# A kernel of attention and experts at its turn to the experts: a step of the softmax changes engine, four steps change place

## The chip, the cores and the metric

The kernel runs on one core of one Trainium2 chip. The metric is the device time of one execution in microseconds (us); three runs gave a median of 504.72 us (504.45 to 505.11). A core has TensorE (PE in the rows; PEld is its weight load), VectorE (DVE), ScalarE (ACT), GpSimd (POOL) and SyncE (SP), each with its own list of instructions, and 16 DMA engines.

## What is computed

Three stages follow one another: linear attention with decay over 2 x 768 tokens and 8 heads of 64; a dense layer `g = h * sigmoid(1.702 h)` between 512 and 2048 columns; and a mixture of 8 experts with one expert for each token. The change lies in the third:

```python
logits = xn @ en.T / tau                 # xn, en: rows scaled to length 1
expert_idx = np.argmax(logits, axis=1)
probs = np.exp(logits - logits.max(-1, keepdims=True))
probs /= probs.sum(-1, keepdims=True) + 1e-09
gate_w = probs[np.arange(N), expert_idx]
for e in range(E):                       # 8 experts, 512 -> 1024 -> 512
    mask = expert_idx == e
    h = np.maximum(x[mask] @ w1[e], 0.0)
    out[mask] = gate_w[mask, None] * (h @ w2[e])
```

## The kernel before

Tokens stand in tiles of 128 rows, twelve in all. All matrix products are made from a high and a low part of each operand (three products for one). The program order of each engine is written out by hand (`manual_schedule`): an engine takes its instructions in the order in which the functions issue them, and waits at an instruction whose operands are not there yet, with all that stands behind it.

Each tile of the dense layer's result is routed. `Batch` does this for one tile, or for two at once (b01, b23, b4 and b5 are the batches of the last six tiles):

- `norm` (L630 to L640): ScalarE squares the row, GpSimd takes the root. `rn` and `pick` (L672 to L706), on VectorE: logits `lg`, maximum, `z`, and the one-hot choice `oh`.
- `tanh` (L708) on ScalarE: the exponential is taken as (1 + t) / (1 - t) with t = tanh(z / 2).
- `gate` (L711): `dn = 1 - t` (L716), its reciprocal (L717), the sum and its reciprocal, which is written beside the token's row (L727).
- `rank` (L729): TensorE counts with `ltri` and `ones` how many tokens chose the same expert earlier (`pr`; it needs `oh`, and the counter `acc` of the batch before), VectorE makes from it the slot `pos`, adds to `acc` (L746) and casts the slot to an integer `pi` (L748).
- `scatter` (L750): GpSimd writes the token's row to its slot in DRAM with an indirect DMA.

`load_slots` (SP) reads the slots of one expert when all scatters have landed, and `emit_xT` (L892) transposes them on TensorE, ScalarE copies the high part (L901), VectorE makes the low part (L902). Expert 0 comes in two pieces: piece 0 has the tokens of the first six tiles and is loaded early, piece 1 the rest. `emit_mm1t` (L922) and `emit_mm2` (L991) are its two products: 12 and 24 matmuls of 512 columns for a piece and a half or a whole; `emit_relut` (L933, `hr`) and `emit_hT` (L940) stand between them.

`emit_tail` interleaves the last tiles of the dense layer, the routing of b01 to b5 and the first product of piece 0, so that TensorE has work while VectorE routes. The last scatter (b5) decides when piece 1 can be loaded; `emit_experts` goes on with the second product of piece 0 meanwhile.

Of the kernel before, what the change touches and what calls it, by code (L numbers as in the profile page):

```python
# [11 lines left out]
I32 = mybir.dt.int32  # L12
U32 = mybir.dt.uint32
AF = mybir.ActivationFunctionType
ALU = mybir.AluOpType
SYNC_DATA = mybir.DependencyInfo(mybir.DependencyClass.Sync, mybir.DependencyReason.DATA)

P = 128
# [33 lines left out]
def attn_moe_moe_kernel(  # L52
# [16 lines left out]
    nc = tc.nc  # L69
# [20 lines left out]
    def psum_h(shape, name):  # L90
        return ps.tile(shape, F32, tag="h", name=name)
# [158 lines left out]
    pos = {}  # L250
# [366 lines left out]
    class Batch:  # L617
# [93 lines left out]
        def gate(self):  # L711

            z = self.z
            dn = self.tile("dn", [P, self.n, E])
            sm = self.tile("sm", [P, self.n])
            nc.vector.tensor_scalar(dn, z, -1.0, 1.0, op0=ALU.mult, op1=ALU.add)  # L716
            nc.vector.reciprocal(dn, dn)  # L717
            if self.n == 1:
                nc.vector.scalar_tensor_tensor(
                    z, z, 1.0, dn, op0=ALU.add, op1=ALU.mult, accum_out=sm  # L720
                )
            else:
                nc.vector.scalar_tensor_tensor(z, z, 1.0, dn, op0=ALU.add, op1=ALU.mult)
                nc.vector.tensor_reduce(sm, z, axis=mybir.AxisListType.X, op=ALU.add)
            nc.vector.tensor_scalar(sm, sm, 1e-9, None, op0=ALU.add)
            for j, i in enumerate(self.ts):
                nc.vector.reciprocal(yrow[self.g, i][:, DM:DM + 1], sm[:, j:j + 1])  # L727

        def rank(self):  # L729
            pr = psum_h([P, self.n, E], f"pr{self.tag}")  # L730
            for j in range(self.n):
                nc.tensor.matmul(pr[:, j, :], ltri, self.oh[:, j, :], start=True, stop=False)
                for before in range(j):
                    nc.tensor.matmul(
                        pr[:, j, :], ones, self.oh[:, before, :], start=False, stop=False
                    )
                nc.tensor.matmul(pr[:, j, :], ones, acc, start=False, stop=True)
            pf = self.tile("pf", [P, self.n, E])
            pos = self.tile("pos", [P, self.n])
            for j in range(self.n):  # L740
                nc.vector.scalar_tensor_tensor(
                    pf[:, j, :], pr[:, j, :], 0.0, self.oh[:, j, :], op0=ALU.add, op1=ALU.mult,
                    accum_out=pos[:, j:j + 1],
                )
            for j in range(self.n):
                nc.vector.tensor_tensor(acc, acc, self.oh[:, j, :], op=ALU.add)  # L746
            self.pi = self.tile("pi", [P, self.n], I32, bufs=4)
            nc.vector.tensor_copy(self.pi, pos)  # L748

        def scatter(self):  # L750
            for j, i in enumerate(self.ts):
# [88 lines left out]
    def split_e(e, kind, n):  # L840
        split_h(e, kind, n)
        split_l(e, kind, n)
# [35 lines left out]
    def tiles(e):  # L878
        return [(0, W - P), (W - P, P)] if e == 0 else [(0, P), (P, SLOTS[e] - P)]
# [34 lines left out]
    def emit_mm1t(a, half, lo=0, hi=None):  # L914
        off, n = tiles(0)[a]
        x = xe[0][:, 2 * KD * off:2 * KD * (off + n)].rearrange("p (k l w) -> p k l w", k=KD, l=2)
        if lo == 0:
            mm1ps[a, half] = (psum_h if a else psum_y)([P, DM], f"m1t_{a}_{half}")
        steps = [(k, s) for k in range(KD) for s in ((0, 0), (1, 0), (0, 1))]
        last = len(steps) - 1  # L920
        for i, (k, (xi, wi)) in list(enumerate(steps))[lo:hi]:
            nc.tensor.matmul(  # L922
                mm1ps[a, half][0:n], x[:, k, xi, :],
                ws[0, 0, k][wi][:, half * DM:(half + 1) * DM],
                start=(i == 0), stop=(i == last),
            )
# [243 lines left out]
    def emit_tail():  # L1170
        rest = list(range(NF - DEFER, NF))
        last = TPG - 1
        b01, b23, b4, b5 = Batch(1, 0, 1), Batch(1, 2, 3), Batch(1, 4), Batch(1, 5)
        where = {0: (b01, 0), 1: (b01, 1), 2: (b23, 0), 3: (b23, 1), 4: (b4, 0), 5: (b5, 0)}
        for i in range(TPG):
            emit_l2(1, rest, i, 0, 5)
            if i == 1:
                emit_xT(0, 0)
            if i > 2:
                b, j = where[i - 1]  # L1180
                b.transpose(j, KD)
            if i == last:
                b23.pick()
                b23.tanh()
                b01.rank()
                b01.scatter()
            emit_l2(1, rest, i, 5)
            emit_y(1, i)
            b, j = where[i]
            b.norm(j)  # L1190
            if i < 2:
                for e in range(E):
                    b01.dot_dve(i, e)
            if i == 4:
                b23.dots_pe()
                b01.rn()
                b01.pick()
                b01.tanh()
                b01.gate()
                b23.rn()  # L1200
        b23.gate()
        b23.rank()
        b23.scatter()
        b4.rn()
        b4.dots_pe()
        b5.transpose(0, KD)
        b4.pick()
        b4.tanh()
        b5.rn()
        emit_mm1t(0, 0, 0, 6)  # L1210
        b4.gate()
        b5.dots_pe()
        b4.rank()
        b4.scatter()
        for n in (2, 3):
            split_h(0, 1, n)
        b5.pick()
        b5.tanh()
        emit_mm1t(0, 0, 6)
        emit_relut(0, 0)  # L1220
        emit_mm1t(0, 1, 0, 4)
        b5.gate()
        b5.rank()
        b5.scatter()
        load_slots(0, 1)
        emit_mm1t(0, 1, 4, 6)
        emit_hT(0, 0)
        split_l(0, 1, 2)
        emit_mm1t(0, 1, 6)
        emit_relut(0, 1)  # L1230

    def emit_experts():
        emit_mm2(0, 0, 0, 6)
        emit_hT(0, 1)
        split_l(0, 1, 3)
        emit_places()
        load_slots(1)
        for n in range(4):
            load_e(1, 0, n)
        for n in range(4):  # L1240
            load_e(1, 1, n)
        emit_mm2(0, 0, 6, 18)
        emit_xT(0, 1)
        emit_mm2(0, 0, 18)
        emit_out(0, 0)
        emit_mm1t(1, 0)
        emit_relut(1, 0)
        emit_mm1t(1, 1, 0, 6)
        emit_hT(1, 0)
        split_e(1, 0, 0)  # L1250
        emit_mm1t(1, 1, 6)
        emit_relut(1, 1)
        for n in range(4):
            load_e(2, 0, n)
        for e in range(E):
            more = e + 1 < E
            if e:
                parts = [(n, i) for n in range(1 if e == 1 else 2, 4) for i in range(2)]
                for f in range(NEF):
                    emit_mm1(e, f)  # L1260
                    if f == 0 and e == 1:
                        emit_out(0, 1)
                    emit_sum(e, f)
                    if f == 0 and e > 1:
                        emit_out(e - 1, 1)
                    if f:
                        emit_relu(e, f - 1)
                    if 1 <= f <= len(parts):
                        split_h(e, 1, *parts[f - 1])
                    if 1 < f <= len(parts) + 1:  # L1270
                        split_l(e, 1, *parts[f - 2])
                    if e == 3 and f == 6:
                        emit_ctl()
                emit_relu(e, NEF - 1)
                if e + 2 < E:
                    for n in range(4):
                        load_e(e + 2, 0, n)
            if more:
                for a in range(NA):
                    emit_xT(e + 1, a)  # L1280
                if e + 2 < E:
                    load_slots(e + 2)
            if e == 0:
                emit_mm2(0, 1, 0, 6)
                emit_hT(1, 1)
                for n in range(1, 4):
                    split_e(1, 0, n)
                split_e(1, 1, 0)
                emit_mm2(0, 1, 6)
            else:  # L1290
                for n in range(4 if more else 0):
                    split_e(e + 1, 0, n)
                emit_mm2(e, 0)
                emit_out(e, 0)
                for n in range(2 if more else 0):
                    split_e(e + 1, 1, n)
                emit_mm2(e, 1)
            if e + 2 < E:
                for n in range(4):
                    load_e(e + 2, 1, n)  # L1300
        emit_out(E - 1, 1)
# [201 lines left out]
```

## Time and profile before

| | |
|---|---|
| median of three runs | 504.72 us (504.45 to 505.11) |
| the profiled execution, its own time | 504.72 us |
| its span, first to last instruction | 503.0 us |
| TensorE busy | 490.8 us (98%) |
| VectorE busy | 356.9 us (71%) |
| ScalarE busy | 268.6 us (53%) |
| GpSimd busy | 108.5 us (22%) |

TensorE is busy through nearly the whole span, so what it waits for is what a change can give or take; the other engines matter where TensorE waits for them. Matmuls overlap in the records (one of 512 columns shows 0.39 us, and the next starts 0.23 to 0.24 us after it), so the step between starts says more than the busy time. The turn to the experts lies between 308 and 346 us.

### The profile page before, as it was taken

What the parts mean: (1) busy time and instruction counts of PE and PEld (TensorE: products, weight loads), DVE (VectorE), ACT (ScalarE), POOL (GpSimd) and SP (SyncE); (2) the same over time, 40 slices, a digit from 0 to 9 for tenths busy, and PEclk for the clock granted to TensorE, in tenths of its full rate; (3) what the DMA queues carried; (4) which work ended last, traced back from release to release, by engine and by line L of the source; (5) the groups of instructions that cost most, each with busy time, mean ns of one, the idle gap of its engine ahead of it and who ended that gap; (6) DMA issues with size and microseconds to landing.
All of it is one profiled execution on the core that took longest, in us unless ns stands there. A gap on an engine that the chain in (4) does not pass through costs nothing. (4 is left out here: it accounts for less than half of the span.)

```text
span 503.0 us, 9454 instructions
## 1 busy us (share of the span) xinstructions
PE 490.8 (98%) x3479; PEld 424.1 (84%) x3480; DVE 356.9 (71%) x850; ACT 268.6 (53%) x576; POOL 108.5 (22%) x153
## 2 busy tenths in 40 slices
PE   8999999999999999999999999999999999999993
PEld 5888898898898899898989988778797988879781
DVE  6788877777687335988789478748956878676640
ACT  2463554554533476434354574538856678567540
POOL 6702111110100023242332337510110111201101
PEclk9999999999999999999999999999999999999998
DMA  8969786864720400121112200369976577865000
GB/s 304 394 188 318 259 267 184 260 211 147 231 85 0 169 0 1 42 71 56 65 63 106 80 2 0 127 235 400 376 263 230 212 227 240 281 207 186 21 9 31
DMA packets 40471, 82.33 MB, mean 164 GB/s; under 512 B 11897, under 2 KB 12409, under 8 KB 40293
## 3 DMA queue, kind: packets, MB, share of 16 engines
q1 hardware_dynamic: 37749, 75.12, 43.9%
q0 software_dynamic: 2240, 6.31, 3.4%
q8 instruction: 28, 0.46, 0.4%
q10 hardware_dynamic: 432, 0.27, 0.2%
q14 instruction: 22, 0.18, 0.1%
HBM read 70.77 MB, written 10.80 MB: 162 GB/s over the span
## 5 line engine op out<-in xcount | busy, mean ns | idle before, releaser
L580 PE MATMUL y<-whl,gg 128*128 128x512 f32 x576 | 141.3, 395 | 0.0
L537 PE MATMUL h<-x,whl 128*128 128x384 f32 x768 | 139.7, 336 | 0.4 <-ACT whl L520 0.2
L537 PEld LDWEIGHTS h<-x,whl 128*128 128x128 f32 x768 | 134.0, 188 | 3.1 <-ACT whl L520 0.6
L580 PEld LDWEIGHTS y<-whl,gg 128*128 128x128 f32 x576 | 106.4, 188 | 21.3
L836 DVE TENSOR_TENSOR wl<-wr,wh 128x1024 fp32r<-128x1024 f32 (+1 forms) x79 | 78.0, 1017 | 5.4 <-ACT wh L831 5.4
L991 PE MATMUL m<-wh,xe 128*128 128x512 f32 (+7 forms) x256 | 80.9, 397 | 0.0
L831 ACT ACTIVATE wh<-wr 128x1024 fp32r<-128x1024 f32 (+1 forms) x79 | 67.4, 890 | 0.4 <-DMA wr<-w 0.4
L955 PE MATMUL m<-xe,wh 128*128 128x464 f32 (+6 forms) x224 | 65.7, 362 | 0.0
L520 ACT ACTIVATE whl<-home 128x512 fp32r<-128x512 f32 x64 | 40.1, 627 | 45.2 <-DVE home L508 44.2
L521 DVE TENSOR_TENSOR whl<-home,whl 128x512 fp32r<-128x512 f32 x49 | 36.1, 736 | 37.3 <-ACT whl L520 37.3
L991 PEld LDWEIGHTS m<-wh,xe 128*128 128x128 f32 (+7 forms) x256 | 42.4, 169 | 15.1 <-DVE xe L944 0.2
L548 ACT ACTIVATE g<-h 128x384 f32<-128x384 f32 x64 | 31.1, 485 | 44.4 <-PE h L537 41.5
L991 PE MATMUL m<-wl,xe 128*128 128x512 f32 (+7 forms) x128 | 50.3, 393 | 0.0
L955 PE MATMUL m<-xe,wl 128*128 128x232 f32 (+6 forms) x224 | 49.8, 262 | 0.0
L646 DVE CUSTOM_DVE_ANT_0 jd<-yr,er 128x512 f32<-128x512 f32 x64 | 48.3, 802 | 0.0
L559 DVE TENSOR_TENSOR gg<-g,gg 128x384 fp32r<-128x384 f32 x64 | 37.4, 585 | 14.3 <-ACT gg L558 14.2
L1005 POOL DMA_INDIRECT out<-o,row x16 | 16.5, 1032 | 136.3 <-ACT o L1002 70.3
L955 PEld LDWEIGHTS m<-xe,wl 128*128 128x128 f32 x224 | 42.1, 190 | 1.2 <-DVE wl L836 0.3
L521 POOL TENSOR_TENSOR whl<-home,whl 128x512 fp32r<-128x512 f32 x15 | 20.9, 1394 | 94.6 <-ACT whl L520 92.8
L964 DVE TENSOR_TENSOR m1r<-m,m1r 128x232 f32<-128x232 f32 (+6 forms) x56 | 20.8, 371 | 28.9 <-ACT m1r L963 28.0
L955 PEld LDWEIGHTS m<-xe,wh 128*128 128x128 f32 x224 | 39.4, 189 | 1.2
L963 ACT ACTIVATE m1r<-m 128x232 f32<-128x232 f32 (+6 forms) x56 | 19.2, 344 | 35.3 <-PE m L955 32.6
(180 smaller groups left out, 537.1 us busy)
## 6 DMA issues: line engine op xcount, KB each, us to landing
wr<-w SPq DMA_DIRECT2D x64, 512.0 KB, 6.2
raw<-w_in SPq DMA_DIRECT2D x16, 512.0 KB, 6.3
raw<-w_out SPq DMA_DIRECT2D x16, 512.0 KB, 6.1
slots<-zrow SPq DMA_DIRECT2D x8, 514.0 KB, 6.0
sl<-slots SPq DMA_DIRECT2D x7, 514.0 KB, 5.7
home<-vn SPq DMA_DIRECT2D x12, 256.0 KB, 6.2
home<-kn SPq DMA_DIRECT2D x12, 256.0 KB, 5.8
home<-kT SPq DMA_DIRECT2D x11, 256.0 KB, 6.5
```

Of the source, the lines that this page charges most:

```text
L520: nc.scalar.activation(t[:, 0], a, AF.Copy)
L521: eng.tensor_tensor(t[:, 1], a, t[:, 0].bitcast(F32), op=ALU.subtract)
L537: nc.tensor.matmul(t, wt[:, wi, k * P:(k + 1) * P], x[:, xi, k, sl], start=(i == 0), stop=(i == 3 * KD - 1),)
L548: nc.scalar.activation(g2, h1.pop((f, hf)), AF.Gelu_apprx_sigmoid)
L559: nc.vector.tensor_tensor(gl, g2, gh.bitcast(F32), op=ALU.subtract)
L580: nc.tensor.matmul(t, a[:, o:o + P], wt[:, wi], start=(f == 0 and n == 0), stop=(f == NF - 1 and n == 2),)
L646: nc.vector.tensor_tensor_reduce(out=jd, in0=yrow[self.g, self.ts[j]][:, 0:DM], in1=route["er"][:, e], scale=1.0, scalar=0.0, op0=ALU.mult ...
L831: nc.scalar.activation(ws[e, kind, n][0][:, o], wr[e, kind, n][:, o], AF.Copy)
L836: nc.vector.tensor_tensor(l[:, o], wr[e, kind, n][:, o], h[:, o].bitcast(F32), op=ALU.subtract)
L955: nc.tensor.matmul(t[:, 0:n], w[:, fs], x[:, k, 0:n], start=(k == 0 and w is wh), stop=(k == KD - 1 and w is wh),)
L964: nc.vector.tensor_tensor(r, t[:, 0:c], r, op=ALU.add)
L991: nc.tensor.matmul(t[0:n], ht[:, hi_lo, f, off:off + n], w[wi][:, o:o + DM], start=(i == 0), stop=(i == last),)
```

## The change

Five edits:

1. `gate`: `dn = 1 - t` is made by ScalarE (an activation Copy with bias 1 and scale -1) and no more by VectorE, in all ten batches.
2. `rank`: the cast to `pi` stands ahead of the additions to `acc`.
3. `emit_tail`: the rank of b5 stands behind six products of `emit_mm1t(0, 1)` and no more behind four; the transposes `emit_hT(0, 0)` still follow the sixth.
4. `emit_experts`: the transposes of piece 1 stand behind 20 products of `emit_mm2(0, 0)` and no more behind 18.
5. `emit_mm1t(1, 0)`: its eight products with the high part of the tokens come first, its four with the low part last.

```diff
             sm = self.tile("sm", [P, self.n])
-            nc.vector.tensor_scalar(dn, z, -1.0, 1.0, op0=ALU.mult, op1=ALU.add)
+            nc.scalar.activation(dn, z, AF.Copy, bias=1.0, scale=-1.0)
             nc.vector.reciprocal(dn, dn)
...
+            self.pi = self.tile("pi", [P, self.n], I32, bufs=4)
+            nc.vector.tensor_copy(self.pi, pos)
             for j in range(self.n):
                 nc.vector.tensor_tensor(acc, acc, self.oh[:, j, :], op=ALU.add)
-            self.pi = self.tile("pi", [P, self.n], I32, bufs=4)
-            nc.vector.tensor_copy(self.pi, pos)
...
         steps = [(k, s) for k in range(KD) for s in ((0, 0), (1, 0), (0, 1))]
+
+        if a and not half:
+            steps.sort(key=lambda step: step[1][0])
         last = len(steps) - 1
...
-        emit_mm1t(0, 1, 0, 4)
+        emit_mm1t(0, 1, 0, 6)
         b5.gate()
         b5.rank()
         b5.scatter()
         load_slots(0, 1)
-        emit_mm1t(0, 1, 4, 6)
         emit_hT(0, 0)
...
-        emit_mm2(0, 0, 6, 18)
+        emit_mm2(0, 0, 6, 20)
         emit_xT(0, 1)
-        emit_mm2(0, 0, 18)
+        emit_mm2(0, 0, 20)
```

ScalarE at the last tiles, before: `z_2` and `z_4` are the tanh of b23 and b4, `yr_5` the copy of the last tile out of PSUM, `junk_5` its squares, `yt_5` its transposed copy, `wh` a split of expert weights, `hr_0` the relu of piece 0.

```order
L709 ACTIVATE z_2_3703<-z_2_3703 128x16
L592 ACTIVATE yr_5_3740<-y_5_2324 128x512
L635 ACTIVATE junk_5_0_3742,ssq_5_3501<-yr_5_3740 128x512
L660 ACTIVATE yt_5_0_3787<-yT_5_0_3782 128x512
L709 ACTIVATE z_4_3793<-z_4_3793 128x8
L831 ACTIVATE wh_1_2_3835<-wr_1_2_3360 128x1024
L831 ACTIVATE wh_1_3_3838<-wr_1_3_3402 128x1024
L709 ACTIVATE z_5_3845<-z_5_3845 128x8
L933 ACTIVATE hr_0_3860<-m1t_0_3804 104x512
```

ScalarE at the same place of the changed kernel (`dn` is the new copy of b23, b4 and b5; `L936` was `L933`):

```order
L709 ACTIVATE z_2_3703<-z_2_3703 128x16
L592 ACTIVATE yr_5_3740<-y_5_2324 128x512
L635 ACTIVATE junk_5_0_3742,ssq_5_3501<-yr_5_3740 128x512
L716 ACTIVATE dn_2_3746<-z_2_3703 128x16
L660 ACTIVATE yt_5_0_3787<-yT_5_0_3782 128x512
L709 ACTIVATE z_4_3793<-z_4_3793 128x8
L716 ACTIVATE dn_4_3811<-z_4_3793 128x8
L831 ACTIVATE wh_1_2_3835<-wr_1_2_3360 128x1024
L831 ACTIVATE wh_1_3_3838<-wr_1_3_3402 128x1024
L709 ACTIVATE z_5_3845<-z_5_3845 128x8
L936 ACTIVATE hr_0_3860<-m1t_0_3804 104x512
L716 ACTIVATE dn_5_3869<-z_5_3845 128x8
```

The copy of b23 stands behind `yr_5` and `junk_5`, which were issued ahead of `gate`, and that of b5 behind the relu `hr_0`; the others follow their tanh directly.

TensorE at the rank of b5 (`pr_5`) and the transposes of piece 0 (`hT_0`), before and then in the changed kernel:

```order
L922 MATMUL m1t_1_3862<-wh_0_0_3073,xe_3542 104x512 x2
L922 MATMUL m1t_1_3862<-wl_0_0_3074,xe_3542 104x512
L922 MATMUL m1t_1_3862<-wh_0_1_3184,xe_3542 104x512
L732 LDWEIGHTS ltri
L732 MATMUL pr_5_3874<-oh_5_3846,ltri 128x8
L737 LDWEIGHTS ones
L737 MATMUL pr_5_3874<-acc,ones 128x8
L922 MATMUL m1t_1_3862<-wh_0_1_3184,xe_3542 104x512
L922 MATMUL m1t_1_3862<-wl_0_1_3185,xe_3542 104x512
L940 MATMUL hT_0_3889<-ident,hr_0_3860 128x104 x4
```

```order
L925 MATMUL m1t_1_3862<-wh_0_0_3073,xe_3542 104x512 x2
L925 MATMUL m1t_1_3862<-wl_0_0_3074,xe_3542 104x512
L925 MATMUL m1t_1_3862<-wh_0_1_3184,xe_3542 104x512 x2
L925 MATMUL m1t_1_3862<-wl_0_1_3185,xe_3542 104x512
L732 LDWEIGHTS ltri
L732 MATMUL pr_5_3876<-oh_5_3846,ltri 128x8
L737 LDWEIGHTS ones
L737 MATMUL pr_5_3876<-acc,ones 128x8
L943 MATMUL hT_0_3889<-ident,hr_0_3860 128x104 x4
```

The rank now follows the sixth product of the half (`wl_0_1`), and the transposes follow the rank with nothing between.

VectorE from the choice of b23 (`oh_2`) on, before and then in the changed kernel:

```order
L703 TENSOR_TENSOR oh_2_3704<-wgt_2_3702,mi_2_3701 128x16
L741 SCALAR_TENSOR_TENSOR pf_0_3719,pos_0_3720<-pr_0_3713,oh_0_3667 128x8 x2
L746 TENSOR_TENSOR acc<-acc,oh_0_3667 128x8 x2
L748 CAST pi_0_3725<-pos_0_3720 128x2
L716 TENSOR_SCALAR dn_2_3746<-z_2_3703 128x16
L717 RECIPROCAL dn_2_3746<-dn_2_3746 128x16
L723 SCALAR_TENSOR_TENSOR z_2_3703<-z_2_3703,dn_2_3746 128x16
```

```order
L703 TENSOR_TENSOR oh_2_3704<-wgt_2_3702,mi_2_3701 128x16
L741 SCALAR_TENSOR_TENSOR pf_0_3719,pos_0_3720<-pr_0_3713,oh_0_3667 128x8 x2
L746 CAST pi_0_3723<-pos_0_3720 128x2
L748 TENSOR_TENSOR acc<-acc,oh_0_3667 128x8 x2
L717 RECIPROCAL dn_2_3746<-dn_2_3746 128x16
L723 SCALAR_TENSOR_TENSOR z_2_3703<-z_2_3703,dn_2_3746 128x16
```

VectorE no longer has `dn`, and its reciprocal is the next instruction behind the counter `acc` of b01, with the rest of b23, b4 and b5 behind it.

## Rows read from the trace of the kernel before

**Rows 1.** The waits of TensorE over the whole span: waited for, us in total, times, longest

```profile
PE xt L892 <- DMA sl<-slots: 0.7, 1, 0.7
```

**Rows 2.** The timeline of TensorE at the turn: start us, us, engine line operation [idle before]

```profile
318.30 0.17 PE L732 MATMUL pr<-oh,ltri 128*128 128x8 bf16 x1
...
320.48 0.40 PE L922 MATMUL m1t<-wh,xe 128*104 128x512 f32 x1
321.01 0.17 PE L732 MATMUL pr<-oh,ltri 128*128 128x8 bf16 x1
...
325.12 0.69 PE L991 MATMUL m<-wh,xe 128*104 128x512 f32 x2
...
327.74 0.39 PE L991 MATMUL m<-wl,xe 128*104 128x512 f32 x1
328.79 0.66 PE L892 MATMUL xt<-ident,sl 128*128 128x128 f32 x4 [0.67 <-DMA sl<-slots]
329.20 0.71 PE L991 MATMUL m<-wh,xe 128*104 128x512 f32 x2
...
330.68 0.69 PE L922 MATMUL m1t<-wh,xe 128*128 128x512 f32 x2
```

**Rows 3.** The timeline of TensorE's weight loads, same columns

```profile
320.71 0.10 PEld L732 LDWEIGHTS <-ltri 128*128 128x128 bf16 x1 [0.29 <-issue]
```

**Rows 4.** The timeline of VectorE

```profile
314.43 0.17 DVE L716 TENSOR_SCALAR dn<-z 128x16 f32<-128x16 f32 x1
314.63 0.25 DVE L717 RECIPROCAL dn<-dn 128x16 f32<-128x16 f32 x1
...
317.74 0.17 DVE L703 TENSOR_TENSOR oh<-wgt,mi 128x8 bf16<-128x8 f32 x1
...
318.77 0.20 DVE L717 RECIPROCAL dn<-dn 128x8 f32<-128x8 f32 x1
...
319.75 0.21 DVE L685 SCALAR_TENSOR_TENSOR lg<-pd,ssq,c_e 128x8 f32<-128x8 f32 x1
...
320.79 0.17 DVE L703 TENSOR_TENSOR oh<-wgt,mi 128x8 bf16<-128x8 f32 x1
...
321.07 0.20 DVE L717 RECIPROCAL dn<-dn 128x8 f32<-128x8 f32 x1
...
321.98 0.15 DVE L748 CAST pi<-pos 128x1 int32<-128x1 f32 x1
```

**Rows 5.** The timeline of ScalarE

```profile
313.62 0.22 ACT L709 ACTIVATE z<-z 128x16 f32<-128x16 f32 x1
314.77 0.60 ACT L592 ACTIVATE yr<-y 128x512 f32<-128x512 f32 x1 [0.94 <-PE y L580]
315.40 0.63 ACT L635 ACTIVATE junk<-yr 128x512 f32<-128x512 f32 x1
315.94 0.19 ACT L635 ACTIVATION_READ_ACCUMULATOR junk<-yr 128x1 f32 x1
...
317.66 1.99 ACT L831 ACTIVATE wh<-wr 128x1024 fp32r<-128x1024 f32 x2
320.59 0.21 ACT L709 ACTIVATE z<-z 128x8 f32<-128x8 f32 x1 [0.94 <-DVE wgt L698]
320.71 0.58 ACT L933 ACTIVATE hr<-m1t 104x512 f32<-104x512 f32 x1
...
329.49 0.60 ACT L901 ACTIVATE xe<-xt 128x512 fp32r<-128x512 f32 x1 [3.68 <-PE xt L892]
```

**Rows 6.** The timeline of GpSimd

```profile
322.92 0.97 POOL L752 DMA_INDIRECT slots<-yr,pi  x1 [0.79 <-DVE pi L748]
```

**Rows 7.** The timeline of SyncE's DMA queue

```profile
326.06 0.37 SPq L872 DMA_DIRECT2D sl<-slots  x1
```

**Rows 8.** The costliest groups of the page: instruction, busy and mean ns, idle before

```profile
L548 ACT ACTIVATE g<-h 128x384 f32<-128x384 f32 x64 | 31.1, 485 | 44.4 <-PE h L537 41.5
```

**Rows 9.** Busy time in a stretch: PE, PEld, DVE, ACT, POOL, granted clock, DMA share, GB/s

```profile
340.00:344.00 4.00, 4.00 (x19) 3.15 (x19) 3.55 (x4) 3.61 (x5) 0.00 (x0) 1.00 1.04 394
```

## The prediction

> **What bounds the kernel now.** I read the waits of TensorE first. Behind the first 100 us it waits once by that view: 0.7 us for the load of the second piece of expert 0 [rows 1]. Since TensorE is otherwise busy to the end, time won or lost there goes into the end one to one. The timeline of TensorE at the turn gives the true size: products start 0.238 us apart (eleven steps from 325.12 to 327.74, [rows 2]), so after the twelfth TensorE was free at 327.74 + 0.24 = 327.98, and the transposes began at 328.79: a wait of 0.81. One wait more is hidden in the busy time: the rank of b5 could have begun when the product of 320.48 was through, 320.72, where its weight load indeed stands [rows 3], and began at 321.01 [rows 2], 0.29 later, when b5's choice of 320.79 (0.17 long) was there [rows 4]. These two waits, 1.10 us, are all that the moves can win.
>
> Then the chain behind the 0.81: VectorE makes b5's slot (`pi`, 321.98, [rows 4]), GpSimd scatters from 322.92 on, waiting for just that [rows 6], SyncE issues the load when the scatter has landed, at 326.06 [rows 7], and TensorE has it at 328.79. From `pi` to the transposes that is 0.94 + 3.14 + 2.73 = 6.81 us with nothing to spare in it.
>
> **The copy on ScalarE.** By itself it costs nothing: VectorE's instruction takes 0.17 with 0.20 to the next [rows 4], a ScalarE instruction of the same 16 columns 0.22 [rows 5]. The copy itself is not in the trace; that row is the nearest, and 0.1 either way would move all that follows by as much.
>
> The Trainium skill ("ScalarE: Activation LUTs", Rules for kernel authors) sends adding and multiplying to VectorE, because of its rate per element. At 8 or 16 columns the rows don't show that difference; by that reason alone the sum would be the gain of the moves (503.95, below) and some hundredths more.
>
> What decides is where the copy stands in ScalarE's list. In the loop of the dense layer (six batches) it stands behind its tanh or behind one gelu more, 0.49 each; VectorE gets it up to 0.5 us late. ScalarE itself waits 41.5 us for TensorE before the 64 gelus [rows 8], and no wait of TensorE lies there, so I take 0; if the cover were gone in all six, at most 3 us, which I hold for very unlikely. At b01 it follows its tanh: 0.
>
> At b23 it does not. The tanh of b23 was done at 313.84, and VectorE's `dn` ran at 314.43. In ScalarE's list of the changed kernel the copy follows the last tile's copy out of PSUM (314.77, held by TensorE) and its squares, whose accumulator is read at 315.94 [rows 5]. A small instruction starts about 0.12 behind the one ahead of it (320.59 to 320.71, [rows 5]), so the copy runs from 316.05 to 316.25, and the reciprocal, 314.63 before, starts at 316.27: 1.64 us late [rows 4]. Everything of b23, b4 and b5 on VectorE is queued behind it.
>
> From that reciprocal to b4's choice it was 314.63 to 317.74, 3.11. The cast ahead of `acc` adds 0.11 here, since it waits for its accumulator where `acc` used to fill the time (an estimate from the step of 0.20 between dependent instructions less what overlaps). So b4's choice begins at 319.49, ends at 319.66, and the rank of b4 on TensorE, 318.30 before [rows 2], runs at 319.72 to 319.80: a new stall of 1.42 to 1.50. I take 1.45. Nothing hides it: the six products behind it belong to the same queue.
>
> The next link gives back a little. VectorE's `dn` of b4 had waited for another instruction before; now its reciprocal follows b4's choice by about 0.35 (three small steps), at 319.84 instead of 318.77: 1.07 late. From there to b5's logits it was 0.98 [rows 4], now 1.05 with the cast's 0.07: 320.89. b5's tanh ran 0.84 behind that (319.75 to 320.59): 321.73. The two weight splits ahead of it in ScalarE's list (1.99 us from 317.66, [rows 5]) now start behind b4's copy at 319.65 and end at 321.64, just in time. Then the relu, 321.85, and behind it b5's copy: the relu takes 0.58, of which the last 0.1 overlaps, so 322.34 to 322.55. The reciprocal of b5 starts at 322.58 instead of 321.07: 1.51 late [rows 4].
>
> **The cast ahead of the counter.** In a batch of one tile the cast waits for its accumulator, and `acc` ran in that gap; it gains between 0 and 0.1 us. I take 0. So `pi` of b5, and with it scatter and load, come 1.51 later: the piece is there at 328.79 + 1.51 = 330.30. At b01 the additions end some 0.17 later, which can hold b23's rank by up to 0.1; the stall at b4's rank swallows it.
>
> **The two moves on TensorE.** Rank behind two products more: b5's choice is ready at 321.93 + 0.17 = 322.10 and the rank's turn comes at 319.75 + 12 x 0.238 = 322.61, so the 0.29 goes. The transposes of piece 0 now come directly behind; their relu is done at 322.43: no wait. Transposes of piece 1 behind two products more: 2 x 0.238 = 0.48 moves in front of the wait.
>
> **The order in the next product.** Before, six products stood between the transposes and it (329.20 to 330.68, [rows 2]). Four products, 0.95, now stand between those transposes (329.20 - 328.79 = 0.41 to the next start) and the first that needs the high part, 1.36 behind the transposes' start. The copy started 0.70 behind it and took 0.60 (328.79, 329.49; rows 2 and 5): 1.30. Just covered, 0 to 0.1 us. The low part is needed from the ninth product on, no more from the second: 0, at best a gain of 0.06.
>
> **The sum.** TensorE reaches the transposes at 327.98 + 1.45 - 0.29 + 0.48 = 329.62; the load comes at 330.30, so a wait of 0.68 stays, and the load's time decides. Against before the transposes are 1.51 later with 0.48 more work done: +1.03. Counted by waits it is the same: 1.45 - 0.29 + (0.68 - 0.81). Behind this nothing absorbs it: TensorE shows no further wait for data that comes earlier than it, and the loads of the next experts are released by the same work. The profiled execution took 504.72 us (503.0 of it the span), the median of the runs shown is 504.72 too: 505.75.
>
> **Bounds of what the trace does not show.** The path from scatter to load is one sample, 3.14 + 2.73. If it shrank by 0.68, the load would be hidden and TensorE alone would count: 1.45 - 0.29 - 0.81 = +0.35, 505.07. If it grew by half a microsecond, +1.53, 506.25.
>
> **Rivals.**
> - *The stall is real, the load catches up* (505.07 to 505.5): the last scatter now stands alone on the DMA engines, further behind that of b4 (whose slot is made at about 320.8). For it: half a microsecond is a small part of 5.87. Against: the last scatter already had nothing behind it. It decides from a path shorter by 0.3 on.
> - *The turn is later and the first experts pay more* (506.1 to 506.5): the weights of the next expert come in a stretch in which the DMA engines are full (share 1.04, 394 GB/s, [rows 9]). If these loads are held longer than TensorE, by 0.3 to 0.5 us, TensorE waits there a second time; a slower landing of the scatter gives the same time. Against: TensorE shows no wait for weights now, and loads and products move by nearly the same.
> - *The copy is no brake, and the moves win* (504.72 - 0.29 - 0.48 = 503.95): the place is b23's reciprocal; the price would be zero if VectorE came no more than about 0.4 us late there, because b4's choice ended at 317.91 and its rank ran at 318.30. For it: both waits that the moves aim at stand in the rows. Against: ScalarE would have to run the copy ahead of an instruction that waits for TensorE until 314.77.
> - *The change does something else*, such as a second table load for the copy: ScalarE's list has only the one at its start, so I give this nothing.
>
> **How the numbers follow.** The forecast (+0.8 to +1.3) gets 0.55, a load that catches up 0.20, later still 0.20, the moves that win 0.05. A difference under 0.2%, 1.01 us, can hardly be told from none here. My forecast lies almost on that line: of its 0.55 I put 0.30 above it. So slower by more than 0.2%: 0.30 + 0.20 = 0.50; within: 0.25 + 0.20 = 0.45; faster 0.05. The range 504.9 to 506.4 leaves out the win, the upper end of the late cases and a rest at the bottom. The forecast's own range is 505.5 to 506.0.
>
> **What would show it.** In the changed profile: the copy of b23 on ScalarE directly behind the read of the last squares, and VectorE idle for some 1.5 us before its reciprocal, waiting for ScalarE; a gap of about 1.4 us on TensorE before the rank of b4, which is not there now; no gap at the rank of b5; the wait for the second piece still there, 0.5 to 0.7 us, with the load issued about 1.5 us later in relation to the last product of the dense layer. The stretch before 308 us should be unchanged. No gap at b4's rank would prove the forecast wrong at its root; a gap with a total under +0.4 would leave the stall right and the load's part wrong.

## The result: 507.63 us, slower by 0.5%

| | before | changed |
|---|---|---|
| median | 504.90 us (4 runs, 504.45 to 505.11) | 507.63 us (4 runs, 506.86 to 507.97) |
| ratio | | 1.0051, interval 1.0039 to 1.0063 |
| profiled execution | 504.72 us | 506.86 us |
| its span | 503.0 us | 505.2 us |
| last matmul starts | 493.77 us | 495.99 us |

The direction was forecast, the size was not: +1.03 us was said, and the medians differ by 2.73. A second set of five runs gave 507.11 (ratio 1.0043, 1.0030 to 1.0056); over all nine the median is 507.23.

The profile after is read in the order of the prediction's steps. The profiled executions already differ by 0.54 us at the last tile's seven products, which start at 312.90 before and at 313.44 after; executions differ by that much from the start (the first products of the attention stand at 4.24 and 4.79, and e5 below, without any copy on ScalarE, has its seven at 313.84). Differences to before below are less this 0.54.

The waits of TensorE over the whole span of the changed kernel (the columns are those of [rows 1]):

```profile
PE xt L892 <- DMA sl<-slots: 1.5, 1, 1.5
PE pr L732 <- DVE ssq L673: 0.9, 1, 0.9
```

The wait of [rows 1] was 0.7 and is 1.5, and there is a new one at the rank of b4. Where the second comes from stands in the timeline of ScalarE after, around the copies of b23 and b5:

```profile
316.48 0.19 ACT L635 ACTIVATION_READ_ACCUMULATOR junk<-yr 128x1 f32 x1
316.57 0.20 ACT L716 ACTIVATE dn<-z 128x16 f32<-128x16 f32 x1
...
322.37 0.58 ACT L936 ACTIVATE hr<-m1t 104x512 f32<-104x512 f32 x1
322.84 0.20 ACT L716 ACTIVATE dn<-z 128x8 f32<-128x8 f32 x1
```

and in the timeline of VectorE after, which answers to [rows 4]:

```profile
316.80 0.25 DVE L717 RECIPROCAL dn<-dn 128x16 f32<-128x16 f32 x1 [1.59 <-ACT dn L716]
...
320.03 0.17 DVE L703 TENSOR_TENSOR oh<-wgt,mi 128x8 bf16<-128x8 f32 x1
...
323.08 0.20 DVE L717 RECIPROCAL dn<-dn 128x8 f32<-128x8 f32 x1 [0.46 <-ACT dn L716]
...
323.98 0.15 DVE L746 CAST pi<-pos 128x1 int32<-128x1 f32 x1
...
324.87 1.22 DVE L836 TENSOR_TENSOR wl<-wr,wh 128x1024 fp32r<-128x1024 f32 x1
```

The copy of b23 stands directly behind the read of the last squares, and VectorE is idle for 1.59 us until it is done; its reciprocal comes 1.63 later than before. b5's copy stands behind the relu, and `pi` comes 1.46 later. So far each step is as forecast. The timeline of TensorE after, which answers to [rows 2]:

```profile
313.44 1.84 PE L580 MATMUL y<-whl,gg 128*128 128x512 f32 x7
...
318.28 1.03 PE L667 MATMUL pd<-embt,yt 128*128 128x8 f32 x8
320.25 0.18 PE L732 MATMUL pr<-oh,ltri 128*128 128x8 bf16 x1 [0.94 <-DVE ssq L673]
...
323.15 0.18 PE L732 MATMUL pr<-oh,ltri 128*128 128x8 bf16 x1
...
329.62 0.63 PE L994 MATMUL m<-wh,xe 128*104 128x512 f32 x2
331.73 0.66 PE L892 MATMUL xt<-ident,sl 128*128 128x128 f32 x4 [1.48 <-DMA sl<-slots]
...
337.31 0.60 PE L943 MATMUL hT<-ident,hr 128*128 128x128 f32 x4
```

The rank of b4 is 1.41 later, with 0.94 idle by the record ahead of it (the view names `ssq`, VectorE's next instruction; what the rank needs is the choice `oh` of 320.03, which ends at 320.20); b5's rank follows its product without a wait. Then the transposes of piece 1 come 2.40 later. The forecast has 1.51 there, so 0.89 has come in between. The scatter of b5 shows where, in the timeline of GpSimd after; the row of before is [rows 6]:

```profile
322.18 0.97 POOL L752 DMA_INDIRECT slots<-yr,pi  x1 [0.73 <-issue]
324.92 2.02 POOL L752 DMA_INDIRECT slots<-yr,pi  x1 [1.77 <-DVE acc L748]
```

Every scatter next to it takes 0.97 to 1.05 us, b5's took 0.97 before, and here it takes 2.02. The load behind it, in the timeline of SyncE's queue, is issued 4.15 after the scatter's start, where [rows 6, 7] have 3.14:

```profile
329.07 0.37 SPq L872 DMA_DIRECT2D sl<-slots  x1
```

From there it takes 2.66 to the transposes, 2.73 before. The scatter itself is the only link that has grown.

### The profile page after: what moved, and what is told of

The parts are those of the page before. It is cut to its first block, busy times and chain, and to the rows that moved or that the text cites. A ratio compares the mean times of both kernels' runs of the same rounds, so it can differ in the third digit from the quotient of the medians.

```text
span 505.2 us, 9455 instructions
## 1 busy us (share of the span) xinstructions
PE 491.7 (97%) x3479; PEld 424.2 (84%) x3480; DVE 356.9 (71%) x840; ACT 269.9 (53%) x586; POOL 111.1 (22%) x153
## 5 line engine op out<-in xcount | busy, mean ns | idle before, releaser
L836 DVE TENSOR_TENSOR wl<-wr,wh 128x1024 fp32r<-128x1024 f32 (+1 forms) x79 | 78.0, 1016 | 5.4 <-ACT wh L831 5.2
L559 DVE TENSOR_TENSOR gg<-g,gg 128x384 fp32r<-128x384 f32 x64 | 38.9, 607 | 13.9 <-ACT gg L558 13.8
L646 DVE CUSTOM_DVE_ANT_0 jd<-yr,er 128x512 f32<-128x512 f32 x64 | 47.2, 785 | 0.0
```

The lines of the kernel that those rows point to most:

```text
L559: nc.vector.tensor_tensor(gl, g2, gh.bitcast(F32), op=ALU.subtract)
L646: nc.vector.tensor_tensor_reduce(out=jd, in0=yrow[self.g, self.ts[j]][:, 0:DM], in1=route["er"][:, e], scale=1.0, scalar=0.0, op0=ALU.mult ...
L836: nc.vector.tensor_tensor(l[:, o], wr[e, kind, n][:, o], h[:, o].bitcast(F32), op=ALU.subtract)
```

## The experiments

Two theories on the 1 us in the scatter. *Held by VectorE*: the split L836, which reads two tiles of 1024 columns, began at 324.87, 0.05 ahead of the scatter, and ended at 326.09; the scatter ended 0.85 after that, as if it had been stopped for the length of the split. Before, by the timeline of VectorE, the split began 0.29 behind the scatter of [rows 6]:

```profile
323.21 1.22 DVE L836 TENSOR_TENSOR wl<-wr,wh 128x1024 fp32r<-128x1024 f32 x1
```

*Something else*: the scatter's own transfers, or the later time as such. Beside that, the stall at b4's rank was to be taken apart from the moves, and a third candidate for the time came up, the clock of TensorE behind that stall.

Two measures from each profiled execution stand beside the medians. "Turn" runs from the start of the last tile's seven products to the first `hT` transposes of piece 1 (313.44 to 337.31 above: 23.87). "To the end" runs from the same start to the last matmul. Both leave out what executions differ in earlier.

| kernel | turn | to the end | median us (runs) | ratio to before, 95% |
|---|---|---|---|---|
| before | 21.98 | 180.87 | | |
| changed | 23.87 | 182.55 | 507.63 (4) | 1.0051 (1.0039, 1.0063) |
| e6, changed again | 23.90 | 182.62 | 507.11 (5) | 1.0043 (1.0030, 1.0056) |
| e1, 1 - t on VectorE | 21.40 | 180.52 | 504.77 (11) | 0.9995 (0.9986, 1.0004) |
| e2, before with the copy alone | 23.17 | 181.87 | 506.62 (7) | 1.0037 (1.0024, 1.0050) |
| e3, b23 alone on VectorE | 21.67 | 180.81 | 504.93 (12) | 0.9998 (0.9989, 1.0007) |
| e4, without the split | 22.88 | 182.16 | 507.36 (7) | 1.0042 (1.0028, 1.0057) |
| e5, before, split early | 22.34 | 181.11 | 505.9 (1) | |
| e7, split later | 24.42 | 184.76 | 508.09 (6) | 1.0058 (1.0044, 1.0072) |
| e8, stall filled | 23.85 | 182.59 | 507.25 (5) | 1.0040 (1.0026, 1.0053) |
| e9, both waits filled | 23.49 | 182.41 | 506.96 (7) | 1.0032 (1.0021, 1.0043) |
| e10, split later, stall filled | 22.99 | 182.94 | 507.26 (5) | 1.0040 (1.0026, 1.0053) |

Each ratio is to executions of the kernel before from the same set, whose medians are 504.90 us (first set), 504.99 (e1 to e4), 504.97 (e5 to e8) and 505.35 (e9, e10); so medians of different sets differ by some tenths for that reason alone.

**e1: the changed kernel with 1 - t back on VectorE** (edits 2 to 5 alone).

```diff
-            nc.scalar.activation(dn, z, AF.Copy, bias=1.0, scale=-1.0)
+            nc.vector.tensor_scalar(dn, z, -1.0, 1.0, op0=ALU.mult, op1=ALU.add)
```

> The changed kernel with its 1 - t back on VectorE; the four moves stay. Theory A (the copy's place on ScalarE makes all of the loss, through the late reciprocal of b23): no gap on TensorE before the rank of b4, no gap at the rank of b5, the wait for piece 1 down from 0.67 to some 0.3 us, and a total of about 504.1, 0.8 below the kernel before. Rival B (the moves cost by themselves, since the transposes of piece 0 now follow the rank with nothing between and only four products cover the copy of piece 1): 505.5 or more with VectorE's reciprocal of b23 on time. If VectorE's split of expert weights starts before the last scatter here, theory A with a held scatter gives up to 0.7 more, 504.8.

The turn is 0.58 shorter than before: the moves do what they aim at. But the total, 504.77, can't be told from before, where 504.1 was expected; the 504.8 of the expectation was meant for a held scatter, and the scatter took 0.97. Why so little of the 0.58 arrives stands under e4.

**e2: the kernel before with edit 1 alone** (the diff above the other way round).

> The kernel before with only the 1 - t on ScalarE; no move. Theory A: the gap before the rank of b4 is there (1.4 us), the rank of b5 waits no more or hardly, the last scatter starts about 1.5 us late, and the total is as high as that of the changed kernel or up to 0.5 above it (507.5 to 508.2), since TensorE has two products less ahead of the wait for piece 1. Rival B: at most 1 us over the kernel before, 505.9.

The turn is 1.19 longer and the ratio 1.0037: the copy alone is a loss, but not the whole of it. The total, 506.62, lies between the two expectations (507.5 or more, 505.9 or less). The timeline of e2, TensorE, GpSimd and VectorE:

```profile
319.89 0.18 PE L732 MATMUL pr<-oh,ltri 128*128 128x8 bf16 x1 [0.82 <-DVE ssq L673]
...
324.49 0.97 POOL L752 DMA_INDIRECT slots<-yr,pi  x1 [1.68 <-DVE pi L748]
324.56 1.22 DVE L836 TENSOR_TENSOR wl<-wr,wh 128x1024 fp32r<-128x1024 f32 x1
```

The stall at b4's rank is there, the long scatter is not: here it began 0.07 ahead of the split. In e1 it was 0.09 ahead. So it took copy and moves together to make the scatter long here. Edit 3 takes two products out from between b5's rank and the transposes that lead to the split, which brings the split from 2.20 behind the rank (before) to 1.71 (e1) and 1.72 (changed). The scatter goes from 1.91 to 1.62 in e1, but only to 1.77 in the changed kernel, where b5's slot waits for its copy.

**e3: only b23's 1 - t back on VectorE.**

```diff
-            nc.scalar.activation(dn, z, AF.Copy, bias=1.0, scale=-1.0)
+            if (self.g, self.ts[0]) == (1, 2):
+                nc.vector.tensor_scalar(dn, z, -1.0, 1.0, op0=ALU.mult, op1=ALU.add)
+            else:
+                nc.scalar.activation(dn, z, AF.Copy, bias=1.0, scale=-1.0)
```

> The changed kernel, with the 1 - t of b23 alone on VectorE and the nine others on ScalarE. Theory A: nearly all of the loss goes, no gap before the rank of b4; what is left is b5's copy behind the relu, 0.4 us on the last scatter, so 504.3 to 504.9. Rival C (the other nine copies cost too, in the loop of the dense layer or by the table of functions): 506 or more.

One batch of ten makes the stall: with it back, the stall at b4's rank is gone and the turn is 0.31 shorter than before. The nine other copies cost nothing that the total shows; the wait of 0.46 for b5's copy remains, and the turn gains 0.27 less than in e1. The long scatter is gone too, but by luck, as the timeline of e3 shows, VectorE and GpSimd:

```profile
323.89 1.28 DVE L839 TENSOR_TENSOR wl<-wr,wh 128x1024 fp32r<-128x1024 f32 x1
323.91 0.97 POOL L755 DMA_INDIRECT slots<-yr,pi  x1 [0.97 <-DVE acc L751]
```

The split is 0.02 ahead here; 0.04 ahead it held the scatter in e8. So e3 tells the cause of the stall, but its total doesn't tell whether b5's copy is free of the risk.

**e4: the changed kernel without the split** (only the scatter's neighbour goes; the low part of these weights is left out).

```diff
-        split_l(0, 1, 2)
+        ws[0, 1, 2][1] = ws[0, 1, 2][0]
```

> The changed kernel without VectorE's split of the third piece of expert 0's second weights (its low part is left out, the products take the high part twice). Theory D (this split, which starts just before the last scatter, holds GpSimd while it makes the scatter): the scatter takes about 1.0 us again and not 2.0, the load of piece 1 is issued 1.0 us earlier, and the total falls by 1.0 to about 506.6. Rival E (the scatter is long for another reason, such as its late place or what the DMA queues still carry): it still takes 2.0 us, and the total stays at 507.6.

The timeline of e4, GpSimd's scatter and three places of TensorE:

```profile
325.08 0.97 POOL L752 DMA_INDIRECT slots<-yr,pi  x1 [1.76 <-DVE acc L748]
...
330.91 0.66 PE L892 MATMUL xt<-ident,sl 128*128 128x128 f32 x4 [0.51 <-DMA sl<-slots]
...
355.46 0.38 PE L958 MATMUL m<-xe,wh 128*128 128x464 f32 x1
356.17 0.99 PE L892 MATMUL xt<-ident,sl 128*128 128x128 f32 x8 [0.32 <-DMA sl<-slots]
```

The scatter is back at 0.97 and the turn 0.99 shorter than in the changed kernel: the split is the cause of the 1 us. But the total did not fall, against what was expected. One reason is the last two rows: some 20 us later the transposes of a later load wait, 0.71 behind the product ahead of them. The same pair in the changed kernel, with the last matmul:

```profile
356.32 0.38 PE L958 MATMUL m<-xe,wh 128*128 128x464 f32 x1
356.54 0.93 PE L892 MATMUL xt<-ident,sl 128*128 128x128 f32 x8
...
495.99 0.39 PE L994 MATMUL m<-wl,xe 128*52 128x512 f32 x1
```

in e1:

```profile
353.72 0.38 PE L958 MATMUL m<-xe,wh 128*128 128x464 f32 x1
354.21 0.99 PE L892 MATMUL xt<-ident,sl 128*128 128x128 f32 x8
```

and before, with the marks of the two measures:

```profile
312.90 1.84 PE L580 MATMUL y<-whl,gg 128*128 128x512 f32 x7
...
334.88 0.60 PE L940 MATMUL hT<-ident,hr 128*128 128x128 f32 x4
...
353.87 0.38 PE L955 MATMUL m<-xe,wh 128*128 128x464 f32 x1
354.22 0.99 PE L892 MATMUL xt<-ident,sl 128*128 128x128 f32 x8
...
493.77 0.39 PE L991 MATMUL m<-wl,xe 128*52 128x512 f32 x1
```

Without a wait the step is 0.22, as after the long turn of the changed kernel. It is 0.35 before, 0.49 in e1, 0.50 in e3 and 0.71 in e4: waits of 0.13, 0.27, 0.28 and 0.49. The view of that tile names the load of the slots as what they end with, in before, e1 and e3 too; it moves in the stretch where the DMA engines are full [rows 9]. So the kernel before already stood at this second limit, and part of a gain at the turn is given back there: of e4's 0.99, 0.39 is left at the end (182.16 against 182.55).

The other reason is probably the clock, though the longest execution is not one of those at a low clock: of the seven executions of e4 three show a mean granted clock of 0.990 to 0.992, at 507.36 to 507.89. Four lie at 0.993 to 0.996: 505.67, 506.61, 506.69 and 507.98.

**e5: the kernel before with the split ahead of the transposes**, which puts it in front of the scatter, without copy and moves.

```diff
-        emit_hT(0, 0)
         split_l(0, 1, 2)
+        emit_hT(0, 0)
```

> The kernel before, with VectorE's split of expert 0's third piece of second weights issued ahead of the low part of the first transposes, so that it runs from about 322.05 to 323.3 and has begun when the last scatter starts at about 322.9. Theory D (a split that has begun holds the scatter to its end): the scatter's instruction takes about 1.2 us (0.85 from the split's end, as in the changed kernel) where it took 0.97, and the load of piece 1 is issued some 0.25 later. Rival E (nothing of the split reaches the scatter): 0.97 as before.

The timeline of e5, VectorE and GpSimd:

```profile
322.99 1.22 DVE L836 TENSOR_TENSOR wl<-wr,wh 128x1024 fp32r<-128x1024 f32 x1
323.85 1.19 POOL L752 DMA_INDIRECT slots<-yr,pi  x1 [0.79 <-DVE pi L748]
```

The scatter starts 0.36 ahead of the split's end at 324.21, takes 1.19 and ends 0.83 behind that end (0.85 in the changed kernel). It is stopped until the split ends, rather than slowed in proportion: overlaps of 0.36 here and 1.17 in the changed kernel cost 0.22 and 1.05, each the overlap less 0.12 to 0.14. That tells a hold from "the later time" or from the transfers. One execution, 505.9, is too little for a total.

**e6: the changed kernel once more.**

> The changed kernel once more, unaltered. The profiled execution of it explained 1.9 us at the turn, the median lies 2.7 above the kernel before, and those of its executions with a lower mean clock are the long ones. Theory F (behind the gap on TensorE the granted clock falls in some executions, and products run at 1.2 GHz for a while): a profile of a long execution has a stretch near the turn in which the clock is 0.5 and steps between products are doubled. Rival G (the rest is spread over the experts' stage, by transfers): clock 1.00 to the last product and steps as before.

Split at 324.78, scatter at 324.83, 2.01 long; the turn 23.90 against 23.87. The hold is no accident of one execution. Theory F is not decided by it: the profile fell on an execution with the clock at 1.00 from 316 to 328 us.

**e7: the split moved behind the second `hT`**, so that it can't meet the scatter.

```diff
         emit_hT(0, 0)
-        split_l(0, 1, 2)
         emit_mm1t(0, 1, 6)
...
         emit_hT(0, 1)
+        split_l(0, 1, 2)
         split_l(0, 1, 3)
```

> The changed kernel, all of it computed, with the same split issued behind the low part of the second transposes, so that VectorE has nothing to do when the last scatter starts. Theory D: the scatter takes 0.97 and not 2.0, the load of piece 1 is issued 1.0 earlier, and the turn, from the last tile's seven products to the transposes of piece 1's first half, takes 22.9 us and not 23.9; the total falls to about 506.6. Rival E: scatter and total unchanged, 507.6.

The scatter took 0.97, and yet the kernel is the slowest of all. The profiled execution shows two reasons. The first, TensorE in stretches of 2 us (busy time, granted clock, DMA share, GB/s):

```profile
318.00:320.00 2.00, 1.83 (x12) 1.00 0.64 237
320.00:322.00 2.00, 1.22 (x6) 0.83 0.34 132
322.00:324.00 2.00, 2.00 (x7) 0.50 0.35 132
324.00:326.00 2.00, 2.00 (x13) 0.81 0.34 132
```

and the timeline of TensorE there:

```profile
320.78 0.18 PE L732 MATMUL pr<-oh,ltri 128*128 128x8 bf16 x1 [0.95 <-DVE ssq L673]
...
321.82 1.05 PE L925 MATMUL m1t<-wh,xe 128*104 128x512 f32 x2
322.68 0.63 PE L925 MATMUL m1t<-wl,xe 128*104 128x512 f32 x1
...
325.25 0.18 PE L732 MATMUL pr<-oh,ltri 128*128 128x8 bf16 x1
```

Behind the stall at b4's rank the clock falls from 2.4 to 1.2 GHz for some 3 us. Three products take 1.29 (321.82 to 323.11 by the next start) instead of 0.69, and from b4's rank to b5's it is 4.47 instead of 2.90: 1.57 us lost. Less these, the turn is 22.85, as expected. The second reason is a new wait of 1.25 at 343.82, which e10 has too and shows more plainly.

**e8: five matmuls of constants in the stall** ahead of b4's rank.

```diff
         b5.dots_pe()
+        keep_warm(5, psum_y)
         b4.rank()
```

> The changed kernel with five more matmuls of constants (512 columns, results not used) ahead of the rank of b4, where TensorE has its gap of 1.4 us; they take about 1.1 us of it. By the work alone nothing changes, since the rank waits for VectorE. Theory F (the gap lowers the clock in some executions): those no longer occur, mean clocks stay at 0.993 to 0.996, and the median falls to about 506.8. Rival G: 507.6 as before.

Turn and scatter (2.02) are as in the changed kernel, so the filling costs nothing. No execution has a mean clock under 0.993. The median isn't lower than e6's, as it should have been: by time alone this run decides nothing.

**e9: both waits filled**, six matmuls ahead of b4's rank and five ahead of the transposes of piece 1.

```diff
+        keep_warm(6, psum_y)
         b4.rank()
...
+        keep_warm(5, psum_y)
         emit_xT(0, 1)
```

> The changed kernel with six matmuls of constants ahead of the rank of b4 and five ahead of the transposes of piece 1, where TensorE waits 1.4 and 1.5 us; results not used. Theory F (the gap ahead of b4's rank lets the granted clock fall in some executions, and the products behind it then run at 1.2 GHz): no execution has a mean clock of 0.992 or less, as in 4 of 9 of the changed kernel, and the median is 506.9, the 1.9 of the turn and nothing more. Rival H (the clock falls for another reason, such as the work of the stages before): low clocks as often as before, median 507.2 to 507.6.

The sixth matmul made both ranks 0.2 later, but not b5's copy. The split follows b5's rank by 1.72 as ever, the scatter by 1.57 instead of 1.77: it came first (325.64, split 325.79) and took 0.97. The second filling outlasted the load, and the turn is 0.61 longer than e4's. No low clock in seven executions. The median meets the 506.9 that was expected, but by luck: that sum had the hold in it and stood on a kernel before at 504.97. Against the 505.35 of its own set e9 is 1.61 longer, and its profile accounts for 1.54 of that.

**e10: e7 with the stall filled.**

> The split behind the second transposes, as before, with the gap ahead of b4's rank filled by five matmuls of constants. Theories D and F together: the last scatter takes 0.97, the turn takes 22.9 to 23.1 us, no execution of 0.992 or less, and the median falls to 505.9 to 506.4. If theory D is right and theory F wrong, low clocks remain and the median stays above 507.

The turn is 1.01 longer than before, as expected, and no execution is at a low clock; but the total stayed at 507.26, 1.91 over before in its set, where the profile to the end has 2.07. The timeline of e10, ScalarE and TensorE behind the turn:

```profile
339.60 1.06 ACT L831 ACTIVATE wh<-wr 128x1024 fp32r<-128x1024 f32 x1 [2.28 <-DMA wr<-w]
340.56 0.58 ACT L936 ACTIVATE hr<-m1t 128x512 f32<-128x512 f32 x1
...
341.19 0.66 PE L943 MATMUL hT<-ident,hr 128*128 128x128 f32 x4 [0.91 <-ACT hr L936]
```

The two splits now stand together ahead of the instructions that find the slots of expert 1 on VectorE; its loads are issued at 332.80 (330.31 before, with the seven products 0.19 earlier), ScalarE waits 2.28 for its weights, and the relu behind that in its list comes too late for TensorE. That is the same fault as the change's own: an instruction behind another that waits.

**The clock, counted.** A mean clock of 0.992 or less showed in 11 of 29 executions of kernels with the open stall (changed and e6 4 of 9, e2 1 of 7, e4 3 of 7, e7 3 of 6), in none of 17 with the stall filled (e8 to e10), in none of 23 without it (e1, e3) and none of 47 of the kernel before. In the changed kernel's nine runs these four have a mean of 507.62, the other five of 506.94. One profile (e7) shows the fall itself; that it is the same in the changed kernel's slower runs is inferred from these counts, since both its profiles fell on executions at full clock. Two things limit the counts. Twelve of the 17 with the stall filled (e9, e10) ran on another chip than e1 to e8, so that on one chip the filling rests on five executions; the contrast with e1 and e3 has no such weakness. And in e7 the three low executions have a mean of 508.88 and the other three of 507.37, 1.51 apart like the fall in its profile, while the changed kernel's are 0.68 apart. Why a fall would cost less there is not shown; one possible reason is that it delays b5's rank, and in e9 a rank 0.2 later was enough to put the scatter in front of the split and spare the hold.

## Why the prediction was right and wrong

- **The copy waits in ScalarE's list: shown.** b23's reciprocal 1.64 late by forecast, 1.63 measured; b4's rank 1.45 and 1.41; `pi` of b5 1.51 and 1.46; b5's rank without a wait. e3 shows that b23 alone makes the stall, e2 that the copy alone is enough for it.
- **The other batches cost nothing: borne out** by e3, whose total is that of before.
- **The moves: shown**, 0.58 at the turn in e1 (0.77 was their price in the rival that they win). In e1 the load still came last, with a wait of 0.41 by the record and only 0.05 earlier than before, so that the 0.29 won at b5's rank ended in the wait for it.
- **"The path from scatter to load is one sample, 3.14 + 2.73": the term that failed.** It was bounded at 0.68 shorter and half a microsecond longer, and taken as it stood; it measured 4.15 + 2.66, 0.94 longer. The scatter was costed at its 0.97 wherever it came to lie, and VectorE's split was not among the instructions whose place against it was looked at, though both rows were in the trace, 0.29 apart. Without the hold (e4) the turn is longer by 0.90, and 1.03 was said: the rest of the sum up to the turn holds. With the 0.89 put in, the sum gives 506.6, which is still short of the 507.63 of the first set; the next points are on that rest.
- **"Behind this nothing absorbs it": wrong for a gain, and 0.13 off for a loss.** The step of 0.35 before the later transposes (353.87 to 354.22) was a hidden wait, which a later turn removes. Turn and this slack give 1.89 - 0.13 = 1.76; from the turn's start to the last matmul it is 1.68.
- **The stall was priced by its length.** The fall of the clock behind it was in no bound. It is no part of the profiled 1.68, and by the counts above it adds some 0.7 in four of nine executions; three of these four lie in the first set, which makes its median 2.73 later rather than the 2.26 of all nine.
- **The rival "later and the first experts pay more"** had the nearest time (506.1 to 506.5) and named a slower landing of the scatter as one way to it. What was slower was GpSimd's instruction and not the landing: from its end to the issue of the load it took 2.17 before and 2.13 after. The rival's own mechanism, a second wait for weights, is not in the changed profile; such a wait did happen in e10, on ScalarE.

What stays open: the five executions at full clock have a mean 1.97 over the median of 504.97 of before, the profile accounts for 1.68. The difference is within the intervals above. In e2 such a rest shows as well: 1.63 by the medians, 1.00 to the end in its profile.

## What to carry to other kernels

An instruction that is moved to an engine with time to spare gets the place in that engine's list, not the spare time: look first at what stands ahead of it and waits. After a shift, look at every pair on VectorE and GpSimd that was close in time, since a few hundredths decided here which of the two went first, and 1 us hung on it. And before you count on a gain, read the steps of the next loads' consumers: a step of 0.35 in a row of 0.22 is a limit that stands right behind the first.

## What the runs showed of the hardware

- **A split on VectorE that begins first stops GpSimd's scatter.** The split's start less the scatter's, and the scatter's length: -0.86, 1.19 (e5); -0.05, 2.02 and -0.05, 2.01 (changed, e6); -0.04, 2.02 (e8); -0.02, 0.97 (e3); +0.07 (e2), +0.09 (e1), +0.15 (e9), +0.29 (before), 0.97 each. Only a split that began 0.04 or more ahead held the scatter. The Trainium skill ("SBUF — State Buffer", Who interferes with whom) says that a VectorE instruction with two SBUF inputs contends with a GpSimd instruction that reads SBUF, and (same page, Summary: rules for kernel authors) that the second one to issue is blocked until the first finishes. With the split first by 0.04 or more, these runs agree. With the scatter first they show less than a block: the split still took its 1.22 (before, e1, e2, e9). In e3, where the split was first by 0.02, the scatter was not held and the split took 1.28.
- **The granted clock fell behind a stall of about 1 us**, to 0.50 for a whole stretch of 2 us (e7), and products took twice their time. The profiles of the changed kernel, e6, e2 and e4 have a stall of 0.82 to 0.95 us at the same place and a clock of 1.00 behind it, so not every such stall brings the fall.
